# Block attention and a gated feed-forward layer: one Silu with the scale beta in place of tanh and a vector operation, beta taken out of w_out, and a reordered output stage

## The chip, the cores and the metric

The kernel runs on one core of a Trainium2 chip. The metric is device time in microseconds. Before the change six runs gave 286.33 to 288.69 us with a median of 287.18 us.

A core has five engines that run their own instruction queues in order: TensorE (PE, with its weight loads listed as PEld), VectorE (DVE), ScalarE (ACT), GpSimd (POOL) and SyncE (SP, here only used to issue DMAs). TensorE writes to PSUM, from where VectorE and ScalarE read.

## The reference

```python
scores = q_c @ k_c.T / sqrt(64)          # per batch, head and chunk of 64 positions
attn   = softmax(scores)
x      = (attn @ v_c)                    # heads side by side: 4608 tokens x 512
h      = x @ w_in                        # 512 -> 2048
g      = h * (1 / (1 + exp(-beta * h)))  # beta: one value for each of the 2048 columns
out    = g @ w_out                       # 2048 -> 512
```

q, k and v have 8 batches, 8 heads, 576 positions and 64 dimensions. All inputs and the output are float32; on chip the matrices are float16, with float32 sums in PSUM.

## The kernel before, in words

The 4608 tokens are taken in nine blocks j of 512. For each block the work is in three stages.

*Attention* of a block is eight chunks of 64 positions, in two groups of four (`emit_sc`, line 134: scores of one group for all heads, 64 small matmuls, then two Exp activations, line 159) and four pairs (`emit_pv`, line 166: 16 matmuls L178 of the exponentials with v, which carries a column of ones for the sum; on VectorE a reciprocal L193 and a multiplication L195; then a transposing DMA L203 on SP that writes a quarter of xt). In the first two blocks xt is transposed by TensorE and copied by ScalarE instead (`emit_xp`, line 207). q and k come in rows and are turned by VectorE (`emit_T`, line 118, four transposes for a batch, two of q and two of k).

*First layer* (`L1`, line 436): 16 tiles m of 128 of the 2048 hidden columns, each four matmuls of 128x512 (L235) into one of four PSUM banks, then `emit_g` (line 243). Swish is there computed with h * sigmoid(beta h) = 0.5 h (1 + tanh(beta h / 2)): ScalarE takes the tanh with the scale beta2 = beta/2 (L246), VectorE adds one and multiplies by h (L249); the factor 0.5 is left to the end. The first tiles of a block are taken in two halves of 256 tokens, so that the first half needs only the first two quarters of xt.

*Second layer*: block 0 takes it plainly (`L2_plain`, line 402: 16 units of four matmuls, which read w_out in four quarters, one quarter each for four units). The other blocks use Strassen's scheme in Winograd's form (`steps_L2`, line 291): seven products `mm[0]` to `mm[6]` of 16 matmuls 128x256 (L308), four of them summed up in one bank A, which ScalarE copies out in between (`take`: u1, u2, u3, L319); `cB`, `cD` and `cC` are VectorE's combinations of a bank with a copied one (L327), of which cB and cD end in a store by SP (L286). The sums of the hidden values that the scheme needs (`emit_sum`) run on VectorE (s1, s2, s4) and GpSimd (s3); the differences of w_out (`emit_tw`, four of them) are made once on GpSimd. Each copy and combination out of PSUM carries the factor 0.5.

The order on every engine is the order in which the program is written (`tc.manual_schedule`). In a steady block j the scores of block j+1 are emitted before tile 14 of the first layer; the rest of its attention stands between the products of the second layer: the list `at` holds pv0, the second scores, pv1, pv2 and pv3, and `go(at)` emits the next of them; `go(tr)` does so for the four transposes of batch j+2, `dve()` for the queued sums. `emit_sum(j, 3, ..)` is emitted at tile 8. At the end of a block GpSimd issues the loads of v for batch j+2 and of q and k for batch j+3.

At the head GpSimd issues all loads (q and k of batch 0 in two halves each, v, w_in in four parts, w_out in four quarters between later q, k and v), SP the four small ones of beta. `emit_idle(n)` (line 217) makes n matmuls of zeros, 16 at first, then 6, 6 and 2 between the steps of the first attention. `bt` is the transpose of beta on VectorE, after which beta2 is made and then the four transposes of batch 0.

Of the kernel before, what the change touches and what calls it, by code (L numbers as in the profile page):

```python
# [8 lines left out]
FP32 = mybir.dt.float32  # L9
FP16 = mybir.dt.float16  # L10
ACTF = mybir.ActivationFunctionType
ALU = mybir.AluOpType
# [3 lines left out]
def kernel(  # L16
# [37 lines left out]
    sg_p = ctx.enter_context(tc.tile_pool(name="sg", bufs=3))  # L54
# [7 lines left out]
    bstage = const.tile([128, 2, 32], FP32)  # L62
    bt = const.tile([128, 2, 32], FP32)
    beta2 = const.tile([128, 2, 32], FP32)
    warm = const.tile([128, 1], FP32)
    zero = const.tile([128, BLK], FP16)
    w_in16 = [big.tile([128, KDM, DFF // 4], FP16, name=f"wi{i}") for i in range(4)]
# [39 lines left out]
    def load_w_out(g):  # L107
        n = NM // 4
        nc.gpsimd.dma_start(
            out=w_out16[:, g * n:(g + 1) * n].rearrange("p m r d -> p m (r d)"),  # L110
            in_=moe_w_out[g * n * 256:(g + 1) * n * 256, :].rearrange(
                "(m p r) d -> p m (r d)", p=128, r=2),
        )

    qT = {}
    kT = {}
# [12 lines left out]
    def T_items(b):  # L129
        return [lambda z=z, w=w: emit_T(b, z, w) for z in range(2) for w in range(2)]  # L130
# [111 lines left out]

    def emit_g(j, m):
        hps = hps_t.pop((j, m))
        sg = sg_p.tile([128, BLK], FP32, tag="sg", name="sg")
        nc.scalar.activation(  # L246
            out=sg, in_=hps, func=ACTF.Tanh, scale=beta2[:, m % 2, m // 2:m // 2 + 1]
        )
        nc.vector.scalar_tensor_tensor(  # L249
            out=gt_t[j][:, m, :], in0=sg, scalar=1.0, in1=hps, op0=ALU.add, op1=ALU.mult  # L250
        )

    def emit_m(j, m):
# [37 lines left out]
    def steps_L2(j, last=False):  # L291
# [24 lines left out]

        def take(name, src):
            sb[name] = u_p.tile([128, 2, HM], FP32, tag=name, name=name)
            nc.scalar.activation(out=sb[name], in_=bank[src], func=ACTF.Copy, scale=0.5)  # L319

        def comb(src, other, keep=None):
            if keep:
                o = u_p.tile([128, 2, HM], FP32, tag=keep, name=keep)
                sb[keep] = o
            else:
                o = osb_p.tile([128, 2, HM], FP32, tag="osb", name="osb")
            nc.vector.scalar_tensor_tensor(  # L327
                out=o, in0=bank[src], scalar=0.5, in1=other, op0=ALU.mult, op1=ALU.add
            )
            return o  # L330

        s_ = lambda n: s_t[j][n - 1]
# [35 lines left out]
        def mm6():  # L368
            if not last:
                prod("A", s_(1), t1, False)  # L370
                o = osb_p.tile([128, 2, HM], FP32, tag="osb", name="o22")
                nc.scalar.activation(out=o, in_=bank["A"], func=ACTF.Copy, scale=0.5)  # L372
                store(j, 1, 1, o)
                o2 = osb_p.tile([128, 2, HM], FP32, tag="osb", name="o12")
                nc.gpsimd.tensor_tensor(out=o2, in0=sb["t"], in1=o, op=ALU.add)  # L375
                store(j, 0, 1, o2)
                return
            for i in range(2):
                pc = ps_p.tile([128, HM], FP32, tag="p", name="oCi")
                for kk in range(NM):  # L380
                    nc.tensor.matmul(
                        out=pc, lhsT=s_(4)[:, kk, i * 128:(i + 1) * 128], rhs=b22[:, kk, :],
                        start=(kk == 0), stop=(kk == NM - 1),
                    )
                o = osb_p.tile([128, HM], FP32, tag=f"oe{i}", bufs=1, name=f"oe{i}")
                nc.vector.scalar_tensor_tensor(
                    out=o, in0=pc, scalar=0.5, in1=sb["t"][:, i], op0=ALU.mult, op1=ALU.add)
# [14 lines left out]
    def L2_plain(j):  # L402
        ops = [ps_p.tile([128, DM], FP32, tag="p", name="ops") for _ in range(4)]

        def part(kk, t):
            nc.tensor.matmul(  # L406
                out=ops[t],
                lhsT=gt_t[j][:, kk, t * 128:(t + 1) * 128],
                rhs=wo(kk),
                start=(kk == 0),  # L410
                stop=(kk == KFF - 1),
            )

        def unit(g, t):
            for kk in range(4 * g, 4 * g + 4):
                part(kk, t)
            if g < 3:
                return
            osb = osb_p.tile([128, DM], FP32, tag="osb", name="osb")
            if t % 2:  # L420
                nc.vector.tensor_scalar_mul(osb, ops[t], 0.5)
            else:
                nc.scalar.activation(out=osb, in_=ops[t], func=ACTF.Copy, scale=0.5)
# [7 lines left out]
    def dve(n=1):  # L431
        for _ in range(n):
            if fill:
                fill.pop(0)()

    def L1(j, hooks={}, nh=2):
# [6 lines left out]
        for m in range(nh, KFF):  # L443
# [9 lines left out]
                fill.extend([lambda w=w, p=p: emit_sum(j, w, p) for w in (1, 2)])  # L453
            if m >= 10 and j > 1:
                dve()

    with tc.manual_schedule():
        load_qk(0, split=True)
# [13 lines left out]
        for g in range(4):  # L472
# [5 lines left out]
        load_v(1)  # L478
        load_w_out(3)
        load_qk(2)  # L480
        emit_tw(1)
        emit_tw(2)
        load_v(2)
        load_qk(3)
        emit_tw(4)
        emit_tw(3)

        emit_idle(16)
        nc.vector.transpose(
            out=bt, in_=bstage.rearrange("p r i -> p (r i)").rearrange("p (i r) -> p r i", r=2)  # L490
        )
        nc.vector.tensor_scalar_mul(beta2, bt, 0.5)
        for f in T_items(0):
            f()
        emit_sc(0, between=lambda: emit_idle(6))
        emit_sc(1, spare=True)
        emit_idle(6)
        emit_pv(0, xbar=False)
        emit_pv(1, spare=True, xbar=False)
        emit_idle(2)  # L500
        emit_xp(0)
        emit_pv(2, xbar=False)
        emit_xp(1)
        emit_pv(3, spare=True, xbar=False)

        L1(0, {-2: lambda: emit_xp(2), -3: lambda: emit_xp(3)}, 4)
        for f in T_items(1):
            f()
        hooks = {
            9: lambda: emit_sc(2),  # L510
            11: lambda: emit_sc(3),
# [9 lines left out]
        for j in range(1, NB):  # L521
            na = j + 1
            hooks = {}
            if na < NB:
                hooks[14 if j > 1 else 15] = lambda: emit_sc(2 * na)
            if j == 1:
                T2 = T_items(2)
                hooks.update({-1: lambda: emit_xp(7), 4: T2[0], 7: T2[1], 10: T2[2], 12: T2[3]})
# [37 lines left out]
            mm[5]()  # L566
            if j < NB - 1:
# [37 lines left out]
```

## Time and profile before

| | |
|---|---|
| runs, median (lowest to highest) | 287.18 us (286.33 to 288.69) |
| the profiled execution, its own time | 287.23 us |
| its span, first to last instruction | 285.3 us |
| tanh, L246, 144 on ScalarE | 97.8 us, 687 ns each |
| (tanh + 1) * h, L249, 144 on VectorE | 97.1 us, 684 ns each |
| Exp of scores, L159, 34 of 128x512 on ScalarE | 18.4 us, 594 ns each |
| hidden matmuls, L235, 656 | 128.5 us |
| dummy matmuls, L220, 30 | 10.8 us |
| loading of an activation table, one | 1.28 us |
| landing of a load of a w_out quarter | 14.4 to 21.4 us after the issue |

The page gives for each engine its busy time; a line of the waits names the engine and line that waited, what it waited for, and the total in us, the number of times and the longest. The chain of work that ended last goes back from the last instruction to what released it; its pieces are shown with start, length, engine, output tile and line. A timeline row gives start, length, engine, line and operation, with the wait ahead of it in brackets.

### The profile page before, as it was taken

To read this page: it belongs to the slowest core of one execution; us is meant where nothing else is said; L and a number is where in the kernel's file an instruction comes from. 1 tells how busy PE (TensorE), PEld (TensorE's weight loads), DVE (VectorE), ACT (ScalarE), POOL (GpSimd) and SP (SyncE) were. 2 spreads that over 40 slices of the span, in tenths; PEclk is the share of its full clock that TensorE was granted. 3 is DMA by queue.
4 is the path that set the end of the run, shared out by engine and by line. 5 is a ranking of instruction groups with operands and counts; after the bars stand their busy time and mean duration, and the time that the engine had idled before them with its cause. 6 is when DMAs were issued, how large, how long until landed. Compare 5 with 4: busy or idle time off the path is not lost.

```text
span 285.3 us, 7958 instructions
## 1 busy us (share of the span) xinstructions
PE 275.7 (97%) x3406; PEld 178.5 (63%) x3406; DVE 214.4 (75%) x385; ACT 142.2 (50%) x223; POOL 116.2 (41%) x114
## 2 busy tenths in 40 slices
PE   8689999999999999999999999999999999999995
PEld 2355444546784688468845884588458845884584
DVE  1657863599988988898889888988788378837943
ACT  2147705675238723772287228732883188317710
POOL 8733266993049104920392039302910251026100
PEclk9799999999999999999999999999999999999999
DMA  6999999990339644973497349823902320242013
GB/s 105 173 207 211 211 181 203 189 179 3 92 96 165 123 53 133 158 132 50 133 149 146 39 126 156 153 57 97 158 0 52 99 75 2 41 110 74 2 37 110
DMA packets 69586, 31.97 MB, mean 112 GB/s; under 512 B 53680, under 2 KB 63920, under 8 KB 69552
## 3 DMA queue, kind: packets, MB, share of 16 engines
q0 software_dynamic: 44960, 18.35, 52.6%
q1 hardware_dynamic: 24448, 12.99, 17.5%
q8 instruction: 26, 0.43, 0.7%
q10 hardware_dynamic: 144, 0.13, 0.1%
q14 instruction: 8, 0.07, 0.1%
HBM read 36.71 MB, written 9.44 MB: 162 GB/s over the span
## 4 chain that ended last, share of the span: by engine, by line
PE 88%; DVE 7%; DMA 2%; ACT 1%; issue 1%; SPq 0%; DVEq 0%
PE hps L235 40%; PE oA L308 20%; PE oD L308 5%; PE oB L308 5%; PE ops L406 4%; PE oC L308 4%; PE sc L150 4%; PE x L178 3%; DVE gt L249 2%; DMA bstage<-in_moe_beta_dram 2%; PE idle L220 1%; DVE qT L122 1%; DVE kT L122 1%; DVE x L195 1%; PE oE L308 1%
## 5 line engine op out<-in xcount | busy, mean ns | idle before, releaser
L235 PE MATMUL hps<-xt,wi 128*128 128x512 f16 (+1 forms) x656 | 128.5, 353 | 0.8 <-ACT xt L215 0.5
L249 DVE SCALAR_TENSOR_TENSOR gt<-sg,hps 128x512 f16<-128x512 f32 x144 | 97.1, 684 | 30.4 <-ACT sg L246 29.9
L246 ACT ACTIVATE sg<-hps,beta 128x512 f32<-128x512 f32 x144 | 97.8, 687 | 25.7 <-PE hps L235 24.4
L235 PEld LDWEIGHTS <-wi 128*128 128x128 f16 x656 | 63.4, 98 | 58.8 <-issue 1.9
L355 POOL TENSOR_TENSOR w<-u,u 128x512 f32<-128x512 f32 x7 | 8.9, 1274 | 105.5 <-ACT u L319 61.1
L308 PEld LDWEIGHTS <-s 128*128 128x128 f16 x496 | 47.3, 98 | 6.2 <-DVE s L270 0.3
L308 PE MATMUL oA<-tw,s 128*128 128x256 f16 x368 | 44.3, 273 | 0.0
L308 PEld LDWEIGHTS <-gt 128*128 128x128 f16 x384 | 36.4, 98 | 6.3
L272 POOL TENSOR_TENSOR s<-gt 128x512 f16<-128x512 f16 x32 | 36.5, 1192 | 5.9 <-DVE gt L249 5.9
L319 ACT ACTIVATE u<-oA 128x512 f32<-128x512 f32 x24 | 14.3, 597 | 46.1 <-PE oA L308 46.1
L159 ACT ACTIVATE et<-sc 128x512 f16<-128x512 f32 x34 | 18.4, 594 | 36.5 <-PE sc L150 36.5
L94 POOL DMA_DIRECT2D vb<-in_v_dram x32 | 27.5, 879 | 7.6 <-DMA wi<-in_moe_w_in_dram 6.0
L195 DVE TENSOR_TENSOR x<-x,rd 128x512 f16<-128x512 f32 x34 | 23.5, 692 | 1.2
L193 DVE RECIPROCAL rd<-x 128x8 f32<-128x8 f32 x34 | 6.9, 203 | 19.1 <-PE x L178 19.1
L122 DVE STREAM_TRANSPOSE qT<-qu 128x576 f32<-128x576 f32 x16 | 19.9, 1244 | 0.0
L122 DVE STREAM_TRANSPOSE kT<-ku 128x576 f32<-128x576 f32 x16 | 19.8, 1238 | 0.0
L150 PEld LDWEIGHTS <-kT 32*64 32x64 f16 x1152 | 11.1, 107 | 9.4 <-issue 6.1
L308 PE MATMUL oB<-w_out,gt 128*128 128x256 f16 x128 | 15.4, 273 | 0.0
L308 PE MATMUL oD<-tw,gt 128*128 128x256 f16 x128 | 15.4, 273 | 0.0
L308 PE MATMUL oA<-w_out,gt 128*128 128x256 f16 x128 | 15.3, 273 | 0.0
L150 PE MATMUL sc<-qT,kT 32*64 32x64 f16 x1088 | 12.6, 194 | 2.7 <-DVE kT L122 2.7
L375 POOL TENSOR_TENSOR o<-t,o 128x512 f32<-128x512 f32 x7 | 8.9, 1268 | 15.4 <-ACT o L372 15.4
(50 smaller groups left out, 191.2 us busy)
## 6 DMA issues: line engine op xcount, KB each, us to landing
out_dram<-osb SPq DMA_DIRECT2D x21, 256.0 KB, 2.2
vb<-in_v_dram POOLq DMA_DIRECT2D x32, 144.0 KB, 5.6
qu<-in_q_dram POOLq DMA_DIRECT2D x7, 576.0 KB, 8.3
ku<-in_k_dram POOLq DMA_DIRECT2D x7, 576.0 KB, 10.3
out_dram<-o SPq DMA_DIRECT2D x14, 256.0 KB, 2.2
wi<-in_moe_w_in_dram POOLq DMA_DIRECT2D x4, 512.0 KB, 12.6
w_out<-in_moe_w_out_dram POOLq DMA_DIRECT2D x4, 512.0 KB, 16.6
qu<-in_q_dram POOLq DMA_DIRECT2D x2, 288.0 KB, 5.4
```

The lines of the kernel that those rows point to most:

```text
L94: nc.gpsimd.dma_start(out=t[64 * hp:64 * hp + 64, 2 * z:2 * z + 2, :, 0:D].rearrange("p s c d -> p (s c) d"), in_=v[b, h0:h0 + 2].rearrang ...
L122: nc.vector.transpose(out=dst[b][:, z].rearrange("p t r e -> p (t r e)").bitcast(FP32).rearrange("p (t r) -> p r t", r=RUN), in_=src[b][:, ...
L150: nc.tensor.matmul(out=sc[a % 2][o0:o0 + 64, z, c, :], lhsT=kk[:, cb * CH:(cb + 1) * CH, e], rhs=qq[:, cb * CH:(cb + 1) * CH, e], start=(e ...
L159: nc.scalar.activation(out=et, in_=sc[s], func=ACTF.Exp, scale=scale)
L195: nc.vector.tensor_tensor(out=yy, in0=src, in1=rr.to_broadcast(shape), op=ALU.mult,)
L235: nc.tensor.matmul(out=hps_t[j, m][:, c0:c1], lhsT=w_r[m // 4][:, 2 * z + e, m // 2 % 2, m % 2, :], rhs=xt_t[j][:, n, c0:c1], start=(n == ...
L246: nc.scalar.activation(out=sg, in_=hps, func=ACTF.Tanh, scale=beta2[:, m % 2, m // 2:m // 2 + 1])
L249: nc.vector.scalar_tensor_tensor(out=gt_t[j][:, m, :], in0=sg, scalar=1.0, in1=hps, op0=ALU.add, op1=ALU.mult)
L272: tt(out=s3[:, lo], in0=g[:, lo, up], in1=g[:, lo, dn], op=ALU.subtract)
L308: nc.tensor.matmul(out=bank[name][:, i, :], lhsT=a[:, kk, i * 128:(i + 1) * 128], rhs=b[:, kk, :], start=(first and i == 0 and kk == 0), s ...
L319: nc.scalar.activation(out=sb[name], in_=bank[src], func=ACTF.Copy, scale=0.5)
L406: nc.tensor.matmul(out=ops[t], lhsT=gt_t[j][:, kk, t * 128:(t + 1) * 128], rhs=wo(kk), start=(kk == 0), stop=(kk == KFF - 1),)
```

## The change

- Swish is one Silu on ScalarE of beta times h, written to float16: beta h sigmoid(beta h). VectorE's instruction L249 is gone.
- That is beta times what is wanted, so the rows of w_out are divided by beta: 16 multiplications in place on VectorE by `binv`, a reciprocal, four for each quarter of w_out. A beta whose square is under 2^-20 is replaced by 2^-10 first. The differences of w_out on GpSimd are emitted after that.
- The factors 0.5 are gone from all copies and combinations out of PSUM.
- The next block's first scores are emitted behind the last Silu of a block (`hooks[KFF]`) and no longer before tile 14 or 15.
- In the output stage pv0 and the second scores stand behind mm[1] instead of mm[0], cB directly behind mm[1], and the pairs pv1 to pv3 one product later each or behind other work of VectorE: pv3 now comes behind mm[4] and cD.
- At the head the dummy matmuls are 4, 5 and 3; the transposes of batch 0 come before the work on beta.

```diff
+    def scale_w_out(g):
+        for kk in range(4 * g, 4 * g + 4):
+            nc.vector.tensor_scalar_mul(wo(kk), wo(kk), binv[:, kk % 2, kk // 2:kk // 2 + 1])
...
     def emit_g(j, m):
         hps = hps_t.pop((j, m))
-        sg = sg_p.tile([128, BLK], FP32, tag="sg", name="sg")
         nc.scalar.activation(
-            out=sg, in_=hps, func=ACTF.Tanh, scale=beta2[:, m % 2, m // 2:m // 2 + 1]
-        )
-        nc.vector.scalar_tensor_tensor(
-            out=gt_t[j][:, m, :], in0=sg, scalar=1.0, in1=hps, op0=ALU.add, op1=ALU.mult
+            out=gt_t[j][:, m, :], in_=hps, func=ACTF.Silu,
+            scale=beta2[:, m % 2, m // 2:m // 2 + 1],
         )
...
-            nc.scalar.activation(out=sb[name], in_=bank[src], func=ACTF.Copy, scale=0.5)
+            nc.scalar.copy(out=sb[name], in_=bank[src])
...
-            nc.vector.scalar_tensor_tensor(
-                out=o, in0=bank[src], scalar=0.5, in1=other, op0=ALU.mult, op1=ALU.add
-            )
+            nc.vector.tensor_tensor(out=o, in0=bank[src], in1=other, op=ALU.add)
...
             if m >= 10 and j > 1:
                 dve()
+        hooks.get(KFF, lambda: None)()
...
+        emit_idle(4)
+        for f in T_items(0):
+            f()
+        nc.vector.transpose(
+            out=bt, in_=bstage.rearrange("p r i -> p (r i)").rearrange("p (i r) -> p r i", r=2)
+        )
+        eps = 2.0 ** -10
+        nc.vector.tensor_tensor(out=bm, in0=bt, in1=bt, op=ALU.mult)
+        nc.vector.tensor_scalar(
+            out=bm, in0=bm, scalar1=eps * eps, scalar2=None, op0=ALU.is_ge)
+        nc.vector.scalar_tensor_tensor(
+            out=beta2, in0=bt, scalar=eps, in1=bm, op0=ALU.subtract, op1=ALU.mult)
+        nc.vector.tensor_scalar_add(beta2, beta2, eps)
+        nc.vector.reciprocal(out=binv, in_=beta2)
+        emit_sc(0, between=lambda: emit_idle(5))
+        emit_sc(1, spare=True)
+        emit_idle(3)
+        emit_pv(0, xbar=False)
+        emit_pv(1, spare=True, xbar=False)
+        emit_xp(0)
...
+        L1(0, {-2: lambda: emit_xp(2), -3: lambda: emit_xp(3)}, 4)
+        scale_w_out(0)
+        scale_w_out(1)
+        for f in T_items(1):
+            f()
+        scale_w_out(2)
+        scale_w_out(3)
         emit_tw(1)
         emit_tw(2)
         load_v(2)
         load_qk(3)
         emit_tw(4)
         emit_tw(3)
...
             if na < NB:
-                hooks[14 if j > 1 else 15] = lambda: emit_sc(2 * na)
+                hooks[KFF] = lambda: emit_sc(2 * na)
...
             mm[0]()
-            dve(2)
-            go(at)
             while fill:
                 dve()
             mm[1]()
-            emit_sum(j, 4, 0)
+            cB()
             go(at)
             go(at)
+            emit_sum(j, 4, 0)
             emit_sum(j, 4, 1)
-            cB()
             mm[2]()
+            go(tr)
             go(at)
-            go(tr)
-            mm[3]()
             emit_sum(j, 4, 2)
             emit_sum(j, 4, 3)
+            mm[3]()
             go(at)
             go(tr)
             mm[4]()
             cD()
+            go(at)
             go(tr)
             mm[5]()
```

More of the change, by code (lines that the diff above doesn't have):

```diff
@@ L53 @@
     s_p = ctx.enter_context(tc.tile_pool(name="s", bufs=1))
-    sg_p = ctx.enter_context(tc.tile_pool(name="sg", bufs=3))
     u_p = ctx.enter_context(tc.tile_pool(name="u", bufs=1))
@@ L64 @@
     beta2 = const.tile([128, 2, 32], FP32)
+    bm = const.tile([128, 2, 32], FP32)
+    binv = const.tile([128, 2, 32], FP32)
     warm = const.tile([128, 1], FP32)
@@ L371, in mm6 @@
                 o = osb_p.tile([128, 2, HM], FP32, tag="osb", name="o22")
-                nc.scalar.activation(out=o, in_=bank["A"], func=ACTF.Copy, scale=0.5)
+                nc.scalar.copy(out=o, in_=bank["A"])
                 store(j, 1, 1, o)
@@ L385, in mm6 @@
                 o = osb_p.tile([128, HM], FP32, tag=f"oe{i}", bufs=1, name=f"oe{i}")
-                nc.vector.scalar_tensor_tensor(
-                    out=o, in0=pc, scalar=0.5, in1=sb["t"][:, i], op0=ALU.mult, op1=ALU.add)
+                nc.vector.tensor_tensor(out=o, in0=pc, in1=sb["t"][:, i], op=ALU.add)
                 r0 = j * BLK + i * 128
@@ L420, in unit @@
             if t % 2:
-                nc.vector.tensor_scalar_mul(osb, ops[t], 0.5)
+                nc.vector.tensor_copy(out=osb, in_=ops[t])
             else:
-                nc.scalar.activation(out=osb, in_=ops[t], func=ACTF.Copy, scale=0.5)
+                nc.scalar.copy(out=osb, in_=ops[t])
             r0 = j * BLK + t * 128
@@ L480 @@
         load_qk(2)
+        emit_idle(4)
[18 more added lines that the diff above has]
+        emit_xp(0)
+        emit_pv(2, xbar=False)
+        emit_xp(1)
+        emit_pv(3, spare=True, xbar=False)
+        L1(0, {-2: lambda: emit_xp(2), -3: lambda: emit_xp(3)}, 4)
[5 more added lines that the diff above has]
+        scale_w_out(3)
         emit_tw(1)
@@ L486 @@
         emit_tw(3)
[L488 to L508, printed above, removed]
         hooks = {
```

## The prediction

> **What bounds the kernel now.** I read the busy shares first, then TensorE's waits, then the chain that ended last, and last the timeline of one steady block and of the head.
>
> ```profile
> PE 275.7 (97%) x3406; PEld 178.5 (63%) x3406; DVE 214.4 (75%) x385; ACT 142.2 (50%) x223; POOL 116.2 (41%) x114
> ...
> PE sc L150 <- DVE kT L122: 2.7, 2, 2.5
> ...
> PE xp L178 <- issue: 0.6, 1, 0.6
> ```
>
> TensorE is busy 97% of the span and waits some 6 us in all, the longest waits ahead of the first real work. The chain of block 4 shows how tight the steady blocks are:
>
> ```profile
> 152.50 0.64 PE sc L150 x64
> 153.14 1.83 PE hps L235 x8
> 154.97 1.75 PE oA L308 x16
> 156.72 0.25 PE x L178 x16
> ...
> 163.68 0.25 PE x L178 x16
> 163.93 1.85 PE oA L308 x16
> 165.78 1.75 PE oC L308 x16
> 167.53 1.75 PE oA L308 x16
> 169.27 12.11 PE hps L235 x64
> ```
>
> Every piece starts where the one before ends, and all are PE. A block repeats after 28.87 us (140.39, 169.27, 198.14). So work taken from VectorE or ScalarE in a steady block is worth nothing; what can be gained lies in the head and in the first Strassen block, where the chain leaves PE:
>
> ```profile
> 57.56 1.17 DVE qT L122
> 58.73 1.71 DVE gt L249 x3
> 60.44 1.16 DVE kT L122
> 61.59 1.71 DVE gt L249 x3
> 63.30 1.16 DVE qT L122
> 64.46 1.11 DVE gt L249 x2
> 65.58 1.17 DVE kT L122
> ```
>
> **The change part by part.** The sum is against the profiled execution: 287.23 us, a span of 285.3 and 1.9 around it; the median of the runs shown is 287.18, practically the same.
>
> *Swish.* Removed: 144 VectorE instructions (L249), 684 ns each, 97.1 us. The 144 tanh (687 ns) become 144 Silu. No row shows Silu; its bounds are the exp row from PSUM to f16 (594 ns) and the tanh row with the same scale pointer (687 ns). I take 687, the nearest row; both are under the 0.86 us in which TensorE makes a tile. In block 1 the four 1.2 us transposes of the batch after next stand between the gt instructions and VectorE is on the chain from 56.9 to 66.7. From the first hidden matmul at 52.02 to 68.07, when the output stage starts, are 16.05 us; 16 half matmuls at 0.108, 56 at 0.216, the four on-chip transposes (0.24) and one score group (0.64) make 14.7, so 1.3 is waiting. Of this 0.24 is the copy of xt, which stays. Gain 1.1. In its output stage (68.07 to 82.64, 14.57 us) a late sum costs another 0.3 against the steady 14.30 (154.97 to 169.27); with VectorE free of gt that goes too. Together 1.4 us.
>
> *Table loads.* The trace has one ACT_TABLE_LOAD for Exp and Tanh together, 1.28 us (0.74 to 2.02), with the next ACTIVATE at 2.03. It doesn't show whether Silu shares that table: between no load and two per block. I take two, some 17 loads more, 22 us on an engine that is half idle. Where they fall, from T = end of the last hidden matmul: last Silu from 0.04 to 0.73, load to 2.05, both exps to 3.15, copy u1 to 3.75. The scores are read by pv0, which now stands behind mm0 and mm1, at 0.64 + 1.75 + 1.75 = 4.14: 1.0 us spare. Going back to Silu: the copy of o22 ends 0.63 after mm6, the load 1.95 after, the first Silu 2.62; TensorE wants that bank back for tile 4 at 1.73 + 2 x 0.86 = 3.46. Hidden, 0.8 spare. Cost 0.
>
> The Trainium skill, "ScalarE: Activation LUTs", section "What ACT_TABLE_LOAD costs", speaks against this: a switch is 1.28 us and a drain of 1.38, 2.66 together. By it the exps would end at about 4.5 and the first Silu at 4.0 after mm6, each 0.3 to 0.6 us too late, and the estimate would be 8 blocks x 0.9, that is 7 us more. This trace shows the 1.28 and no drain behind it, though nothing was running ahead of it.
>
> *The reordered output stage.* Matmuls stay the same, but the last attention product (pv3: 16 matmuls, L193 and L195 on VectorE, one transposing DMA on SP) moves from behind mm3 to behind mm4 and behind cD, in VectorE's queue and in SP's. Before, its xt had over 2 us spare. Now, counted from the end of mm4 in the chain: u3 is copied from 0.10 to 0.70 (the copy starts later than the 0.03 of before since pv3 now follows on PE), cD starts 0.73, L193 1.34, L195 1.57, ends 2.26, the DMA is issued at 2.29 and lands 2.4 later: 4.69. TensorE needs it at 0.25 + 1.85 + 1.75 + 0.87 (eight half matmuls) = 4.72. Nothing is left for the semaphore (0.05 to 0.1 in other rows). I put 0.05 us into each of blocks 1 to 7: 0.3 us. Low end 0. High end: the transposing DMA follows cD's store on SP. Where it did so in block 5 it took twice the time to issue:
>
> ```profile
> 191.36 0.38 SPq L286 DMA_DIRECT2D out_dram<-osb  x1
> 191.84 2.40 SPq L203 DMA_TRANSPOSE xt<-x  x1
> 194.34 1.20 SPq L203 DMA_TRANSPOSE xt<-x  x1
> ```
>
> It ended 2.88 after the store began. With the store at 1.42 that is issue to 4.30 instead of 3.49: 0.8 us a block, 5.6 in all. I stay at the low end: the same pair in block 1 (store at 76.05, transposing DMA at 76.68) took 1.21, and in the slow cases an instruction fetch of about 1 us lay on one DMA engine just then (queue q8 at 191.84, 220.52 and 249.24). The rest of the move is hidden: cB one step earlier is 0.61 us of VectorE ahead of pv0's L193, whose xt is due 9 us later; the sums of mm2 are ready by 1.6 for a use at 5.03, mm5's by 9.1 for 11.33; the transposes for the next batches fit before cD (VectorE free at 11.27, cD due at 11.8).
>
> *Head.* Queries and keys no longer wait on VectorE for beta (bt and its halving, 0.47 us), which landed at 6.76; ku's second half lands at 10.6, so its transpose ends near 11.86 whatever is ahead. The second scores start then, not at 12.86 behind six dummies of 0.43. After that the exps (1.08) would be done at about 13.7 and three dummies replace six. But the last quarter of v, issued at 6.10, takes 8.8 us to land: 14.9. So the first pv ends near 15.1 instead of 15.53: 0.4 us, bounds 0.35 and 1.0 (the latter if the 0.57 us "issue" gap of the waits goes too). Of the first 16 dummies 4 remain; the 12 stood in time in which TensorE waits for keys until 9.6 anyway, and the clock had fallen again by then, so they cost and bring nothing. The six small operations on beta (0.2 each by L492, 1.2) lie between 11.9 and 13.7 on an idle VectorE.
>
> *Scaling w_out.* 16 multiplications of 128x512 f16 in place. No row shows one: at least the 195 ns of L492 (128x64), at most the 0.41 of a two-source f16 operation of that size (L268). I take 0.27, the memset of the same bytes (L459). The last quarter of w_out lands at 44.8 (issue 30.38, 14.4 to landing), when POOL's second difference starts (44.96). VectorE has scaled it by 44.96 + 4 x 0.27 = 46.0; TensorE asks at 46.19 less the head's gain, and pv4's L193, which queues behind the scaling, ran at 46.39. So 0.4 of head gain survives; at 0.41 each nothing, at 0.2 each 0.6. POOL's differences and the loads behind them (v and qk of later batches) shift by 1 us; tw4 and tw3 then end near 63 and the POOL sums near 67.5, their first uses are after 73. Removing the factors 0.5 changes no duration: L195 as TENSOR_TENSOR has 692 ns, L327 684 to 690.
>
> Sum: 287.2 - 1.4 - 0.4 + 0.3 = **285.7 us**.
>
> **Rivals.**
> 1. *The last xt is late in every block* (slower). Place: SP's queue behind cD's store. For it: the three rows above; against: block 1's pair. Price 7 x 0.8 instead of 0.3: 285.7 + 5.3 = 291.0. It decides from 0.5 us a block on: 7 x 0.5 = 3.5 turns -1.8 into +1.7.
> 2. *The clock falls in the head.* By the table of stages the granted clock was 0.87 from 9.0 to 9.5, 0.50 from there to 12.5 and full from 13: it fell some 2.3 us after the last of the first dummies ended (7.15) and stayed down for 3.4. With 12 dummies for 30, TensorE is less than half busy between 13 and 16; if the clock falls again at about 16.3 for as long, the hidden matmuls from 18.5 on run at half speed for 1 us or a little more, up to 1.0 us lost, and the 0.4 go. 285.7 + 1.4 = 287.1: no change. Against it: no gap of the new head is as long as 2.3 us. The Trainium skill, "TensorE: Matmul & The Clock Gate", part 1, lets the clock fall only after an idle window of some 3.4 us, by which the gaps of the head would cost nothing; here it fell sooner.
> 3. *Table switches come through* at about the price of a second load (1.28 more each): exps end at 4.43 for 4.14, the first Silu at 3.90 for 3.46; 0.29 + 0.44 over 8 blocks is 5.8, 291.5. Only the absence of a drain in the one load seen speaks against it.
> 4. *Better*: the "issue" gap goes, 0.2 per multiplication, no stall for xt: 284.9.
>
> **How the numbers follow.** A run of this kernel can tell about 0.5%, 1.4 us, so faster begins under 285.7. Chances: forecast 0.43, rival 1 0.16, rival 2 0.24, rival 3 0.07, better 0.10. The forecast's own range, 284.9 to 286.4, straddles that line; I count 0.36 of its 0.43 as faster, since two of its three unknown prices (scaling, late xt) have most of their room downwards. Faster 0.46, same 0.07 + 0.24 = 0.31, slower 0.23. The range for 8 in 10 runs from 284.4 to 289.6: below it a little under 0.1, above it the two slow rivals where most blocks stall; a rival 1 in some blocks lies inside.
>
> **What would show it.** Right: chain of the block from 52 to 68 all PE; 18 table loads of 1.28, none followed by a PE wait; the block's period still 28.87. Wrong: a PE wait on L235 for xt or a period above 29.3 (rival 1), PE waits on L178 for et or on L235 for a Silu (rival 3), a granted clock of 0.5 beyond 13 us (rival 2), PE waiting on w_out's scaling near 45.

## The result and the profile after

The changed kernel is slightly slower: a median of 288.95 us over 20 runs (288.68 to 289.27), and 287.53 us over the 46 runs of the kernel before that were made beside it. The ratio is 1.0041 with a 95% interval of 1.0027 to 1.0055. The forecast was 285.7, in a range from 284.4 to 289.6. The profiled execution took 288.94 us with a span of 287.0, so it can stand against the one before (287.23, span 285.3).

The page's first part and TensorE's waits after the change:

```profile
PE 273.3 (95%) x3388; PEld 177.6 (62%) x3388; DVE 140.6 (49%) x261; ACT 161.7 (56%) x240; POOL 117.1 (41%) x114
...
PE x L183 <- issue: 0.6, 1, 0.6
PE sc L155 <- ACT et L164: 0.5, 2, 0.3
```

VectorE lost 74 us of work, TensorE lost none of its useful matmuls, and the time did not fall: the first line is an average over the span, and as before it tells nothing of where a microsecond goes. Two rows are to be kept in mind: an "issue" wait of 0.6 us stands at L183 as before the change, but is now the attention product of another place, and the scores wait for exponentials, which they did not before.

Cutting both chains at the same events shows where the time went:

| from the chains, start of | before | after | lost since the row above |
|---|---|---|---|
| the plain output stage of block 0 | 34.15 | 34.59 | +0.44 (since the start: head and first layer of block 0) |
| block 1's first hidden matmul | 52.02 | 54.12 | +1.66 (plain output stage) |
| block 2's first hidden matmul | 82.64 | 83.61 | -1.13 (block 1) |
| block 8's first hidden matmul | 255.89 | 257.50 | +0.64 (six steady blocks) |
| end of the span | 285.3 | 287.0 | +0.1 (block 8) |

Block 1 gave nearly the gain that the forecast had for it. It was more than eaten by the stage ahead of it, the plain output stage of block 0, at which the prediction had looked for one thing only, the scaling of w_out. This is the chain through that stage (start, length, engine, tile and line):

```profile
42.49 0.71 PE sc L155 x64
...
43.31 1.21 issue
44.52 1.09 ACT et L164 x2
...
45.66 0.70 PE sc L155 x63
46.36 0.97 PE ops L405 x4
47.33 0.15 PE x L183 x3
47.48 0.58 issue
48.06 0.41 PE x L183 x13
```

Before, these scores began at 41.92, the second scores at 44.40 and the attention product (16 matmuls of L178) ended at 46.37. Now they begin at 42.49, 45.66, and the product ends at 48.46, 2.1 us late: 0.57 was lost ahead of the first scores, 0.69 between the starts of the first and the second, and 0.78 in the product itself, whose 16 matmuls stop after the third for 0.58 us in which nothing that the profile shows is waited for, and start again slowly.

The second loss is a table load. The timeline of ScalarE and VectorE in that stage (start, length, engine, line, operation; in brackets the wait ahead of it):

```profile
39.06 3.00 DVE L118 TENSOR_SCALAR w_out<-w_out,binv 128x512 f16<-128x512 f16 x4
...
43.23 1.28 ACT L164 ACT_TABLE_LOAD   x1 [7.92 <-PE sc L155]
44.52 1.08 ACT L164 ACTIVATE et<-sc 128x512 f16<-128x512 f32 x2
```

ScalarE stood idle for 7.92 us and could have loaded the table in any of them. But the load stands directly ahead of the Exp and runs only when the scores for which that Exp waits are there. The first row bears on the loss ahead of the first scores: four multiplications of w_out that take 3.00 us together. The line's own view shows that one of them is not like the others (durations are shortest, median, longest in ns):

```profile
L118 DVE TENSOR_SCALAR w_out<-w_out,binv x16: 334/346/2218, 27.7 to 45.3; 128x512 f16<-128x512 f16 x16
```

The one of 2218 ns is the first of the third quarter, 39.06 to 41.27. GpSimd's difference of w_out ran just then:

```profile
37.02 4.09 POOL L284 TENSOR_TENSOR tw<-w_out 128x2048 f16<-128x2048 f16 x1
```

It ended at 41.11, 0.16 ahead of the multiplication. So the third quarter of w_out, which the ninth unit of this stage (of 16) reads, is ready at about 41.2. In this profile TensorE arrives there at nearly the same time, so that no wait shows; the experiments separate the two. The Trainium skill, "SBUF — State Buffer", section "Who interferes with whom", says that VectorE and GpSimd share a pair of ports as a lock held for a whole instruction, and names `tensor_scalar` among the operations that can need it; the row agrees, 2.2 us for 0.35 while GpSimd was at work and 0.35 for the others.

The steady blocks, by the chain of block 4:

```profile
141.56 13.95 PE hps L240 x72
155.51 0.64 PE sc L155 x64
...
166.70 0.25 PE x L183 x16
166.95 1.85 PE oC L310 x16
168.80 1.75 PE oA L310 x16
170.55 13.93 PE hps L240 x72
```

All is TensorE still, but the period went from 28.87 to 28.99 (141.56 to 170.55; 28.98 on average, the 0.64 of the table over six blocks). The hidden stage's pieces hold a small wait that the list of all waits shows: the weight loads wait 1.5 us in seven blocks, 0.2 at most, of which the matmuls feel 0.11 a block.

```profile
PEld L240 <- DMA xt<-x: 1.5, 7, 0.2
```

### The profile page after: what moved, and what is told of

Its sections match the earlier page's. It is cut to its first block, busy times and chain, and to the rows that moved or that the text cites. A ratio compares the mean times of both kernels' runs of the same rounds, so it can differ in the third digit from the quotient of the medians.

```text
span 287.0 us, 7722 instructions
## 1 busy us (share of the span) xinstructions
PE 273.3 (95%) x3388; PEld 177.6 (62%) x3388; DVE 140.6 (49%) x261; ACT 161.7 (56%) x240; POOL 117.1 (41%) x114
## 4 chain that ended last, share of the span: by engine, by line
PE 90%; DMA 3%; DVE 2%; issue 2%; ACT 2%; POOL 1%; DVEq 0%; POOLq 0%; ACTq 0%
PE hps L240 43%; PE oA L310 20%; PE oD L310 5%; PE oB L310 5%; PE oC L310 5%; PE sc L155 4%; PE ops L405 4%; PE x L183 3%; DMA ku<-in_k_dram 3%; PE xps L217 1%; DVE x L200 1%; PE oE L310 1%; PE idle L225 0%; ACT L250 0%; POOL qu L85 0%
## 5 line engine op out<-in xcount | busy, mean ns | idle before, releaser
L250 ACT ACTIVATE gt<-hps,beta 128x512 f16<-128x512 f32 x144 | 95.7, 687 | 17.8 <-PE hps L240 17.1
L270 DVE TENSOR_TENSOR s<-gt 128x512 f16<-128x512 f16 x32 | 17.6, 551 | 80.1 <-ACT gt L250 80.1
L274 POOL TENSOR_TENSOR s<-gt 128x512 f16<-128x512 f16 x32 | 37.5, 1228 | 4.8 <-ACT gt L250 4.8
L321 ACT COPY u<-oA 128x512 f32<-128x512 f32 x24 | 14.1, 588 | 37.0 <-PE oA L310 37.0
L272 DVE TENSOR_TENSOR s<-s,gt 128x512 f16<-128x512 f16 x32 | 17.8, 555 | 1.1
L372 ACT COPY o<-oA 128x512 f32<-128x512 f32 x7 | 4.1, 585 | 23.2 <-PE oA L310 23.2
L329 DVE TENSOR_TENSOR osb<-oB,u 128x512 f32<-128x512 f32 x8 | 5.5, 692 | 20.8 <-PE oB L310 20.8
## 6 DMA issues: line engine op xcount, KB each, us to landing
qu<-in_q_dram POOLq DMA_DIRECT2D x2, 288.0 KB, 5.6
```

The lines of the kernel that those rows point to most:

```text
L250: nc.scalar.activation(out=gt_t[j][:, m, :], in_=hps, func=ACTF.Silu, scale=beta2[:, m % 2, m // 2:m // 2 + 1],)
L270: tt(out=s1[:, lo], in0=g[:, lo, dn], in1=g[:, hi, dn], op=ALU.add)
L272: tt(out=s2[:, lo], in0=s1[:, lo], in1=g[:, lo, up], op=ALU.subtract)
L274: tt(out=s3[:, lo], in0=g[:, lo, up], in1=g[:, lo, dn], op=ALU.subtract)
L321: nc.scalar.copy(out=sb[name], in_=bank[src])
```

## The experiments

The theory after the result: the 1.4 us are a sum of small causes with places of their own, a gain of 1.1 in block 1 against the table load and the stop in the plain output stage, VectorE's held multiplication, and the late xt. The rival, the second one of the prediction: the clock of TensorE falls in the head, since the dummies are fewer. There was something for it. In the profile after, five dummies of 128x512 take 2.31 us and eight half matmuls (of 256 columns) of the first layer 1.87 us, where the profile before has 1.05. A head with 1.05 is called warm in what follows, one with 1.87 cold:

```profile
9.05 2.31 PE L225 MATMUL idle<-zero 128*128 128x512 f16 x5
...
18.51 1.87 PE L240 MATMUL hps<-xt,wi 128*128 128x256 f16 x8 [0.31 <-ACT xt L220]
```

The first three experiments undo one cause each in the changed kernel, the fourth puts the fewer dummies alone into the kernel before, the fifth is the first three together. The kernel before ran beside every experiment, with medians of 287.19 to 287.24 us, against 287.53 beside the changed kernel. The changed kernel itself was not run again, so a difference to its 288.95 us can be off by some 0.3 us; what places each cause is the profiles.

**All dummies back.**

```diff
-        emit_idle(4)
+        emit_idle(16)
...
-        emit_sc(0, between=lambda: emit_idle(5))
+        emit_sc(0, between=lambda: emit_idle(6))
...
-        emit_idle(3)
+        emit_idle(6)
         emit_pv(0, xbar=False)
         emit_pv(1, spare=True, xbar=False)
+        emit_idle(2)
         emit_xp(0)
```

> The changed kernel with the 16, 6, 6 and 2 dummy matmuls of before at the head. Theory A (the changed head runs cold: too few matmuls to bring TensorE's clock up before about 20 us): the single matmuls after 13 us are at full speed again, eight half matmuls of the hidden layer take 1.0 instead of 1.87 us, the plain output stage starts about 0.5 us earlier than 34.6, time 288.4 against 288.95. Rival B (the head is set by the landing of v and by VectorE's chain, the clock costs nothing): plain output stage at 34.6 as before, time 288.9.

Measured: 288.33 us, ratio to the kernel before 1.0025 (1.0001 to 1.0050), 0.62 under the changed kernel. The eight half matmuls took 1.05 again and the plain output stage began at 33.13 instead of 34.42 in the timeline. But 1.0 of these 1.3 us went into a new wait:

```profile
41.17 1.16 PE L405 MATMUL ops<-w_out,gt 128*128 128x512 f16 x4 [0.97 <-DVE w_out L118]
...
47.10 0.32 PE L183 MATMUL x<-vb,et 64*64 64x65 f16 x16
```

The first row is the ninth unit, held by the scaling of w_out until 41.17. The first scores begin at 42.33 for 42.49, a gain of 0.16. The rest of the gain is in the second row: the attention product that stopped for 0.58 us runs in one piece, and block 1's long run (the 64 hidden matmuls that the chain shows as one piece, 55.45 in the changed kernel) begins at 54.52. So the dummies' warm clock is not what gained. They do one other thing: they are 18 more matmuls in TensorE's instruction stream. The row of the DMA queue that brings instructions, for the stretch from 45 to 46 us in the changed kernel (packets, MB, share of that stretch on 16 engines):

```profile
q8 instruction: 1, 0.02, 5.6%
```

In this experiment that packet is not there, and one lies between 38 and 39:

```profile
q8 instruction: 1, 0.02, 6.0%
```

The stop would then be a wait for instructions, which are brought in portions, so that where TensorE runs out depends on the number of instructions ahead. That was a guess from the place of two packets, and the sixth experiment tests it.

**The Exp table loaded early.** A 128x1 Exp, whose result is not used, behind the last Silu of block 0.

```diff
         L1(0, {-2: lambda: emit_xp(2), -3: lambda: emit_xp(3)}, 4)
+        nc.scalar.activation(out=warm, in_=warm, func=ACTF.Exp, scale=1.0)
```

> The changed kernel with one 128x1 Exp on ScalarE behind the last Silu of block 0, so that the table of Exp is loaded while ScalarE has nothing to do, not when the first scores of block 1 are there. Theory A (the 1.28 us load lies on the path in block 0's output stage): load at about 35.3, exps of the first group start at 43.2 instead of 44.5, no wait of the second scores for them, block 1 starts 0.9 to 1.2 us earlier than 54.1, time about 288.0. Rival B (that stage is set by the scaling of the last quarter of w_out, 44.5 to 45.7, and by VectorE's share of pv): at most 0.3 us earlier, 288.7.

Measured: 289.15 us, ratio 1.0070 (1.0049 to 1.0091): no gain, and not the 288.0 of theory A. Yet the load did move, and the exponentials come 1.4 us earlier:

```profile
35.36 1.28 ACT L507 ACT_TABLE_LOAD   x1
...
43.14 1.09 ACT L164 ACTIVATE et<-sc 128x512 f16<-128x512 f32 x2 [6.29 <-PE sc L155]
...
46.40 0.22 PE L183 MATMUL x<-vb,et 64*64 64x65 f16 x3
47.81 0.31 PE L183 MATMUL x<-vb,et 64*64 64x65 f16 x13 [1.20 <-issue]
```

The product began 0.9 us earlier than in the changed kernel, and its stop grew from 0.58 to 1.20: the stop ends at 47.81 for 48.06. Two waits ended at nearly the same time, and to take one away gives only the distance to the next.

**The last attention product ahead of cD.**

```diff
             mm[4]()
-            cD()
             go(at)
+            cD()
             go(tr)
```

> The changed kernel with pv3 emitted ahead of cD instead of behind it; its place among TensorE's matmuls stays. Theory A (xt of the second half lands some 0.1 us late since cD, which waits for u3, and its store stand ahead of it): no wait of the weight loads for xt, the period of a block 28.87 instead of 28.99, 7 blocks give 0.7 us, time 288.2. Rival B (the gap of 0.11 a block comes from the later scores or table loads): the period stays at 28.99, time 288.9.

Measured: 288.16 us, ratio 1.0026 (1.0003 to 1.0048), 0.79 under the changed kernel. The chain has the old period of 28.87 back, and the waits for xt are gone:

```profile
83.62 13.83 PE hps L240 x72
...
112.49 13.83 PE hps L240 x72
...
141.35 13.83 PE hps L240 x72
```

Seven blocks by 0.11 is 0.75, nearly the whole gain. This run bears on the rival as well, by chance. Its head has the few dummies of the changed kernel, but in its profile it ran at full clock (the eight half matmuls took 1.05), and its plain output stage began at 32.91, 1.5 us earlier than in the changed kernel. The long run of block 1's hidden matmuls began at 55.46; in the changed kernel with its slow clock it began at 55.45. The microsecond and a half that this head gained does not reach block 1, since the third quarter of w_out is ready at 41.3 in both.

**The fewer dummies alone, in the kernel before.**

```diff
-        emit_idle(16)
+        emit_idle(4)
...
-        emit_sc(0, between=lambda: emit_idle(6))
+        emit_sc(0, between=lambda: emit_idle(5))
...
-        emit_idle(6)
+        emit_idle(3)
...
-        emit_idle(2)
```

> The kernel before with only its dummies changed, to 4, 5, 3 and none. Theory A (clock): TensorE stays at half speed to about 20 us, hidden matmuls of block 0 end 0.4 to 0.9 us later than 34.15, time 0.5 us above the kernel before. Rival B (what was forecast: fewer dummies let the first attention come earlier): 0.3 to 0.5 us below it.

Measured: 287.04 us, ratio 0.9992 (0.9961 to 1.0023), with runs from 286.36 to 288.50: no difference. Fewer dummies alone don't make the kernel slow. The profiled execution (286.56) had a warm head, its plain output stage at 33.27 for 34.15 in the chain, and since w_out is not scaled there, 0.8 us of that reached the end of the span (284.5 for 285.3). That fits the spread of the runs: 286.3 to 289.6 where the head passes through, 288.7 to 289.3 in the changed kernel, where it doesn't. It is one profile of each, so it is an indication.

**The first three together.**

```diff
-        emit_idle(4)
+        emit_idle(16)
...
-        emit_sc(0, between=lambda: emit_idle(5))
+        emit_sc(0, between=lambda: emit_idle(6))
...
-        emit_idle(3)
+        emit_idle(6)
...
+        emit_idle(2)
...
+        nc.scalar.activation(out=warm, in_=warm, func=ACTF.Exp, scale=1.0)
...
             mm[4]()
-            cD()
             go(at)
+            cD()
```

> The changed kernel with the dummies of before, the early Exp of the second run and pv3 ahead of cD, all together. Theory A (clock, table load, late xt, and the place where TensorE's instruction queue runs dry add up): block 1's long run of hidden matmuls starts at 53.6 to 53.9 against 55.45, the period is 28.87, time 286.6 to 286.9 against 288.95. Rival B (the single runs shared one bound, so that they don't add): 287.5 or more.

Measured: 286.75 us, ratio 0.9982 (0.9965 to 0.9998), 2.20 under the changed kernel. The single gains were 0.62, none and 0.79, together 1.4. The 0.8 on top fits the early table load, which has room once the stop is out of its way: in the chain of the last experiment, which is this kernel, block 1's long run begins at 53.85, with the dummies alone at 54.52.

**Eighteen tiny matmuls instead of the dummies.** As many instructions as the first experiment adds, but of 64 columns; all 18 take 1.17 us, in time in which TensorE waits. They compute nothing that is used.

```diff
         emit_idle(4)
+        d = ps_p.tile([128, BLK], FP32, tag="p", name="idle")
+        for _ in range(18):
+            nc.tensor.matmul(out=d[:, 0:64], lhsT=zero[:, 0:128], rhs=zero[:, 0:64], start=True, stop=True)
```

> The changed kernel with 18 more matmuls of 64 columns behind the first 4 dummies (1 us of work in time in which TensorE waits), so that TensorE has as many instructions ahead of the first block as before, with the clock as cold as in the changed kernel. Theory A (the gap of 0.58 to 1.2 us in pv4, put down to issue, is TensorE's instruction queue waiting for a fetch, and its place goes by the number of instructions ahead): no such gap in pv4, but one in the head near pv3, and block 1's long run starts 0.5 to 0.9 us earlier than 55.45, time 288.0 to 288.4. Rival B (pv4 waits at that place for something else, a load or an exp): the gap stays at 47.5 to 48.1, time 288.9.

Measured: 288.40 us, ratio 1.0024 (0.9999 to 1.0049), 0.55 under the changed kernel, as with the dummies. The stop is not in the output stage any more; one of 0.92 us lies in the head:

```profile
17.98 0.25 PE L183 MATMUL xp<-vb,et 64*64 64x65 f16 x7 [0.92 <-issue]
```

The instruction packet of 45 is again between 38 and 39, where TensorE does not stop, and the long run of block 1 begins at 54.66 for 55.45, though the first scores are where they were (42.47). The head did not stay cold as was expected: in this profile the eight half matmuls took 1.05, so that this run alone does not separate the number of instructions from the warmth. The third and the eleventh do: with few matmuls and a warm head the third has the stop (0.58 us, from 47.48), with all dummies and a cold head the eleventh has none (its product takes 0.36 us from 46.49). So it is the matmuls ahead, not the warmth, that decide where TensorE stops. When TensorE gets there counts too: the seventh and eighth runs have as few matmuls ahead, reach the product at 49.09 and 48.34, after the end of the stop in the others, and do not stop. That the packets are the cause is read from their places in time only. In the head the stop costs nothing in this kernel, as the ninth unit waits for w_out anyway (1.1 us in this run). The kernel before had it there as well (0.57 us, the issue wait of the prediction's first fence); the change, by taking 18 matmuls away, brought one onto the path.

**VectorE's 144 operations back.** An operation of the removed kind behind each Silu, whose result is not used.

```diff
+        junk = sg_p.tile([128, BLK], FP16, tag="sg", name="sg")
+        nc.vector.scalar_tensor_tensor(
+            out=junk, in0=gt_t[j][:, m, :], scalar=1.0, in1=hps, op0=ALU.add, op1=ALU.mult
+        )
```

> The changed kernel with 144 VectorE instructions of the removed kind added (PSUM and f16 in, f16 out to a tile that nobody reads; each holds its PSUM bank until it is done). Theory A (a steady block is bound by TensorE alone, only block 1 gained from VectorE's relief): the period stays within 0.05 of 28.99, block 1 from its start to its output stage takes 1.0 us more, the whole 0.9 to 1.3 us: 290.1. Rival B (VectorE's time counts in every block): the period grows by 0.2 or more, 290.8 or more.

Measured: 292.64 us in four runs, ratio 1.0172 (1.0120 to 1.0224), more than the 290.1 of theory A and in the range of rival B. But its chain shows which blocks care; these are the starts of blocks 2 and 3:

```profile
85.94 13.96 PE hps L241 x72
...
114.93 13.96 PE hps L241 x72
```

The period is 28.99, as without them, where rival B asked for 0.2 more: in the steady blocks the removed operations are worth nothing, but for one pair (below). Block 1 takes 30.64 (55.30 to 85.94) for 29.49 in the changed kernel and 30.62 in the kernel before, so the removed operations were worth 1.1 us there. In the plain output stage they cost more than they did before the change, since the scaling of w_out now queues behind them: that stage began at 36.17, after a wait of 1.8 for w_out, and block 1 1.2 us later than in the changed kernel. And one pair of steady blocks took 58.70 (201.91 to 260.61) instead of twice 28.99, 0.7 lost in one wait of the timeline:

```profile
232.44 0.83 PE L241 MATMUL hps<-xt,wi 128*128 128x256 f16 x6 [0.66 <-DMA xt<-x]
```

An instruction packet of another queue (q14) lay between 230 and 231, while that xt was under way. With pv3 behind cD there is no room for it. It is one case, so that the packet is the cause is not shown. These three places, 1.2, 1.1 and 0.7, are the 3.2 us by which the span grew (290.2 for 287.0).

The run also bears on the multiplication that took 2.2 us. Here the operations put back delay the scaling, and VectorE comes to the third quarter only when GpSimd's difference (38.08 to 42.16) is over; no multiplication of w_out takes more than 392 ns:

```profile
38.08 4.08 POOL L289 TENSOR_TENSOR tw<-w_out 128x2048 f16<-128x2048 f16 x1 [0.96 <-DVE w_out L119]
...
L119 DVE TENSOR_SCALAR w_out<-w_out,binv x16: 277/347/392, 35.8 to 45.5; 128x512 f16<-128x512 f16 x16
```

**The next scores back before tile 14 or 15.**

```diff
-                hooks[KFF] = lambda: emit_sc(2 * na)
+                hooks[14 if j > 1 else 15] = lambda: emit_sc(2 * na)
```

> The changed kernel with the next block's first scores back ahead of tile 14 (15 in block 1). Theory A (moving them is what Silu's own table asks for): two more table loads in each of 8 blocks, 2.56 us of ScalarE ahead of the last two Silus, which then hold PSUM banks and the second half of the values: 0.5 to 2 us a block, 293 to 305. Rival B (ScalarE has room for two more loads): the same time within 0.5 us.

Measured: 295.86 us in two runs, ratio 1.0281 (1.0235 to 1.0327). The chain of a steady block leaves TensorE:

```profile
97.34 0.68 ACT gt L250
...
99.34 1.09 ACT et L164 x2
100.44 1.28 ACT L250
101.74 1.27 ACT gt L250 x2
...
103.06 1.16 PE oB L310 x9
```

Two table loads and the exponentials stand between two Silus, 3.7 us, and TensorE waits for the last two tiles: the period is 29.93 (85.08, 115.01, 144.92). Two loads a block are harmless only because the scores were moved.

Up to block 1 this run is the changed kernel once more, with a still colder head: the granted clock reads 0.50 from 18 to 22 us, and the plain output stage begins at 35.73. That is late enough to pass the third quarter of w_out: the first scores are at 43.50 for 42.49. The product then runs without a stop, and block 1's long run begins at 55.69 for 55.45. So a cold head can reach block 1, by 0.24 us here.

**ScalarE scales the third quarter.** The fifth experiment's kernel, with the third quarter of w_out on ScalarE, which is idle there.

```diff
-        scale_w_out(2)
+        for kk in range(8, 12):
+            nc.scalar.activation(out=wo(kk), in_=wo(kk), func=ACTF.Copy, scale=binv[:, kk % 2, kk // 2:kk // 2 + 1])
```

> The fifth run's kernel (dummies, early Exp, pv3 ahead of cD) with the third quarter of w_out scaled by ScalarE, which is idle then, instead of VectorE, whose first multiplication of that quarter took 2.2 us, until GpSimd's first difference of w_out (37.0 to 41.1) was over. Theory A (that multiplication waits for the GpSimd operation and pins the third quarter's matmuls at 41.2): they start when the second quarter's are done, near 40.0, and block 1 comes 0.5 to 1.0 us earlier than without: 286.0 to 286.3 against 286.75. Rival B (the last quarter of w_out, which lands at 44.8, and the exchange between TensorE and VectorE in the pv steps set block 1's start): 286.6 to 286.8.

Measured: 285.71 us, ratio 0.9943 (0.9921 to 0.9965). This is faster than both kernels, and 1.04 under the fifth experiment, more than theory A had expected.

```profile
36.97 4.08 POOL L284 TENSOR_TENSOR tw<-w_out 128x2048 f16<-128x2048 f16 x1
38.29 2.57 ACT L514 ACTIVATE w_out<-w_out,binv 128x512 f16<-128x512 f16 x4 [2.32 <-DMA w_out<-in_moe_w_out_dram]
...
41.43 0.71 PE L155 MATMUL sc<-qT,kT 32*64 32x64 f16 x64
...
45.51 0.32 PE L183 MATMUL x<-vb,et 64*64 64x65 f16 x16
```

The four multiplications take 2.57 us together, 0.64 each, beside the same 4.08 us of GpSimd, the ninth unit no longer waits for w_out, the first scores are at 41.43 for 42.42 in the timeline and the product at 45.51 for 47.26. Block 1's long run begins at 53.15 for 53.85 in the fifth kernel, 0.7 earlier. What holds it now is the last quarter of w_out, as rival B had it and as the prediction had looked for; the chain goes from its landing over its scaling and the division of the product that queues behind it:

```profile
30.38 14.73 DMA w_out<-in_moe_w_out_dram
...
45.13 1.14 DVE w_out L118 x4
...
46.42 0.70 DVE x L200
...
47.17 0.32 PE x L183 x16
```

**The Silu table loaded early, too.** A 128x1 Silu in the head, so that the first Silu does not come behind a load.

```diff
         emit_sc(1, spare=True)
+        nc.scalar.activation(out=warm, in_=warm, func=ACTF.Silu, scale=1.0)
```

> The ninth run's kernel with one 128x1 Silu on ScalarE behind the exps of the head, so that Silu's table is loaded before the first hidden tile is there. Theory A: the wait of tile 4 of block 0 for the first Silu (0.24 to 0.27 us) goes, and where nothing later pins the stage, the whole is 0.2 us faster than the ninth run. Rival B (pinned later): the same time within 0.1 us.

Measured: 285.78 us, ratio 0.9957 (0.9935 to 0.9979): no difference from the ninth, 0.15 us at block 1's long run (53.00 for 53.15). The 0.27 that tile 4 of block 0 waits in the changed kernel for its bank behind that load are not worth an instruction.

**The fifth kernel once more**, for its chain.

> The fifth run's kernel once more, for a profile. Theory A: third quarter's matmuls start at 41.2 behind a multiplication of 2.2 us on VectorE, no wait of the second scores for the exps, no gap in pv4, block 1's long run from 53.6 to 53.9, period 28.87, span near 284.8. Rival B: one of these waits is still there.

Measured: 286.69 us, span 284.7. All dummies were there, and still the clock was down at the first layer (the granted clock reads 0.50 from 18 to 20 us); VectorE's scaling was held as in the changed kernel:

```profile
17.99 1.89 PE L240 MATMUL hps<-xt,wi 128*128 128x256 f16 x8
...
38.98 3.00 DVE L118 TENSOR_SCALAR w_out<-w_out,binv 128x512 f16<-128x512 f16 x4
...
42.34 0.71 PE L155 MATMUL sc<-qT,kT 32*64 32x64 f16 x64
```

The first scores are at 42.34, within 0.2 of the changed kernel and of the first, second, third and sixth runs, warm head or cold; only where the plain output stage itself began after 35.7, in the seventh and eighth, did they come later. From there the exponentials come without a load, the product runs without a stop, block 1's long run begins at 53.85 for 55.45, and the period is 28.87.

## Why the prediction was wrong

By its own steps, in their order:

- *Swish, -1.4.* Right in mechanism, 0.3 too large. Block 1 gained 1.13, and the seventh experiment, which gives the work back, puts its time at 30.64, before 30.62. Silu took the 687 ns taken for it, and in the steady blocks the removed work was indeed worth nothing.
- *Table loads, cost 0.* This step failed, though not where the prediction looked. There are 18 loads of 1.28 us, and the two of a steady block are hidden: no PE wait follows them, and the activation after a load starts 0.01 behind it. The Trainium skill, "ScalarE: Activation LUTs", section "What ACT_TABLE_LOAD costs", would add a drain of 1.38 us to each; no load of this trace shows one. What the prediction left out is that block 0 has no Strassen stage to hide them in. There the second scores wait for the exponentials of the first, and the load of 1.28, tied to its Exp, put 0.69 us on the path. The same list of loads, walked through block 0 as it was through a steady block, would have shown it.
- *Reordered output stage, 0.05 a block.* Right in mechanism: xt lands a little behind its use. The size is 0.11 a block by the periods and 0.79 in all by the third experiment, against 0.3 forecast; the bound of 0.8 a block did not come about, since the transposing DMA behind the store was issued in 1.19 us in every block.
- *Head, -0.4.* The parts came out (first pv at 14.85 instead of 15.21, first hidden matmul at 18.51 instead of 18.93), but the first layer began with matmuls at half speed, and the plain output stage came 0.44 late. This is the second rival's mechanism. It still did not decide: up to about 1.5 us the head's time is lost or gained ahead of the third quarter of w_out, which does not move; the eighth run shows a head late enough to pass it, and 0.24 us of that at block 1.
- *Scaling w_out, 0.27 each, at no cost while the head's gain lasts.* The size was near (0.35), and the wait was looked for at the last quarter, against the landing of its load. It came at the third, where one multiplication takes 2.2 us beside GpSimd's difference, and 0.35 where the two do not meet (seventh run). With the table load and the stop already undone, taking it off VectorE was worth 1.04, 0.7 of it at the start of block 1; then the last quarter is the limit that the prediction had described.
- *Dummies cost and bring nothing.* As work they don't: the fourth experiment shows no difference, and the clock was up with few of them (third) and down with all of them (eleventh). As instructions they do, and the prediction had no term for that: with 18 fewer a stop of TensorE lies in an attention product on the path instead of in the head, 0.55 to 0.6 us.

The sum, then, is -1.1 from block 1, +0.7 from xt, and +2.1 in the head and the plain output stage, where table load, stop and scaling lie one behind the other and each hides part of the next. The forecast was of 285.7 and the ninth experiment, in which these three and the xt are mended, measured 285.71. That they agree so closely is partly luck: by its profile block 1 gave 1.13 for the 1.4 of the forecast, its start came 0.20 earlier than before (51.82 for 52.02) for the 0.4 of the head, and xt cost nothing for 0.3. Most of the gain that the change holds was read, but what it puts in its way was not.

What stays open: why the clock of the head falls in some runs and not in others. The granted clock does not always show it: it reads 0.50 in the eighth and eleventh runs, but 1.00 in the profile after, while the matmuls take nearly twice their time. It also stays open whether the stop is a wait for instructions.

## What to carry to other kernels

Cost a new operation in every stage in which it occurs: here 15 of the 18 table loads cost nothing, and the one in the irregular stage put 0.69 us on the path. Where a table must be switched, a tiny activation of the coming function behind the last one of the old sends the load ahead of the wait, and two functions that alternate should be kept in long runs. When several causes end at nearly the same time, undoing one shows little; undo them together before one is called harmless.

## What was not expected of the hardware

- A table load does not run ahead of its activation's wait: idle 7.92 us, then the load. With an activation of one column ahead, the load was done at 36.64 and the exponentials began at 43.14.
- Beside GpSimd's 128x2048 difference in float16 one 128x512 multiplication of VectorE took 2.22 us instead of 0.35, ending 0.16 after it; ScalarE doing the same multiplications beside it took 0.64 each.
- TensorE stopped for 0.6 to 1.2 us in the midst of 16 small matmuls; with 18 matmuls of 64 columns more at the very beginning there was no stop at 48 us but one at 17, and the kernel was 0.55 us faster.
- The dummies at the head don't secure the clock: with 30 of them it was down at 18 us in one run (1.89 for eight half matmuls), with 12 it was up in another (1.05).
